# Group sums of the first sequence's v: additions of halves on VectorE in place of sums over a strided axis

## The chip, the cores and the metric

The kernel is one program on one core of a Trainium2 chip. The metric is its time on the device in microseconds (us), the median of the runs. The engines go by short names: TensorE is PE, VectorE is DVE, ScalarE is ACT, GpSimd is POOL, and SyncE is SP, whose queue issues nearly all of the kernel's DMAs.

## The reference

Three layers in a row, in float32: an attention with two parts, a gated MLP and a second MLP. One part of the attention works on means of four neighbouring positions, the other on a band of seven positions around each query.

```python
# 4 batches, 8 heads, 576 positions, 64 channels a head
q_d, k_d, v_d = (t.reshape(B, H, S // 4, 4, D).mean(axis=3) for t in (q, k, v))
out_up = np.repeat(sm_attn(q_d, k_d, v_d), 4, axis=2)      # softmax attention, scale 1/8
scores = scale * np.matmul(q, k.transpose(0, 1, 3, 2))
scores = np.where(np.abs(pos[:, None] - pos[None, :]) < 4, scores, -1e9)
x = out_up + softmax(scores) @ v                           # then to 2304 tokens x 512
g = x @ w_gate                                             # 512 x 1536
x = (g / (1 + np.exp(-g)) * (x @ w_val)) @ w_out           # 1536 x 512
h = x @ w_in                                               # 512 x 2048
out = (np.maximum(h, 0) + alpha * np.minimum(h, 0)) @ w_out2   # 2048 x 512
```

The change touches v_d, the means of four rows of v, for the first of the four batches (the first sequence). The kernel holds them as sums and puts the factor of 1/4 in later.

## The kernel before

**Tiling.** The tokens are cut into 8 blocks of 288, half a sequence each, and the 8 heads into NP = 4 pairs. A half unit n is one block and one pair; there are 32, of which units 0 to 7 (NPRO = 8), the first sequence, run as a prologue. Units 0 to 3 hold the first half of the sequence; n below 4 therefore also names the pair.

**One half unit** goes through these steps, each a function:
- a_T (lines 306 to 334) transposes q and k so that channels lie on partitions and sums groups of four positions; for n = 0 DVE does the latter (lines 327 and 334), for pairs 1 to 3 POOL.
- a_QK (lines 360 and 364) multiplies q and k for the band and for the means; a_EXP (lines 394 and 403, on ACT) takes exponentials, a_NRM divides by the sums (line 427 on ACT for the means).
- a_vd makes vs, the sums of four rows of v, on up to 72 partitions: for n below 4 on DVE, one reduction for each half f of the sequence (line 344), two in a pair, eight in all. In the tile vd a partition holds four rows of 64 channels side by side for each head and half; the reduction reads it in an order in which the four rows are the innermost axis, so neighbouring reads are 64 elements apart. For the later sequences POOL does it by additions of halves (lines 347 and 348), in place in vd and then into vs.
- a_PT (lines 441 and 444) turns the attention weights around, and a_PV (line 461) multiplies them with vs and (line 465) with vw, the windows of v for the band. The windows are copied on the chip's memory into vwin (line 260 and its neighbours) and loaded from there; vw lies in the tile qv. Then ACT scales the product of the means by 1/4 (line 469, the tile is a part of qs), DVE adds both parts (line 470), ACT makes xh, a rounded copy (line 474), and POOL the rest xl (line 475).

The four pairs of the first half have a PSUM bank pair each (att, y0, y1, gv), and units 4 to 7 take over the first three when these are read out.

**The MLPs.** Each product is three matmuls of float32 parts in fp32r (lines 488 to 490: high by high, high by low, low by high). The first MLP has 12 slices j of d_ff, each with a gate, a value and an out weight (g0, v0, o0 and so on; raw_152, raw_154 and raw_156 are those of j = 0, raw_172 to raw_176 those of j = 2, raw_178 to raw_182 those of j = 3, raw_913 to raw_917 those of j = 4). Weights come as 64-bit numbers and are prepared in w_split: two ACT operations (lines 129 and 137), one on DVE (139), a rounding copy on ACT (142) and a subtraction on POOL (143), all 128x512. In block 0 the products of slice j stand behind the preparation of its weights. For a slice, g is projected (m_g), ACT takes a tanh (527), DVE multiplies (528), v is projected (m_v), DVE multiplies again (534), ACT rounds (537), POOL takes the rest (538), and m_y multiplies with the out weight, one slice later. After 8 blocks the second MLP follows (lines 605 to 627).

**Order.** The queues of all five engines are filled by a scheduler. It simulates the program with costs of its own and puts the instructions of each engine in the order in which they come up there. So an instruction with another cost can move others on all queues. A few of them are bound by hand: preparations to instructions of the attention (K's gD, gP, gA), and the copies into vwin for the later sequences to given weight loads. Tiles of the prologue lie in the slots of weights of j = 4 to 11, whose loads therefore wait until the tiles have been read. Once these preparations are over, the products follow one another with the attention of the later blocks in between.

Of the kernel before, what the change touches and what calls it, by code (L numbers as in the profile page):

```python
# [14 lines left out]
AX = mybir.AxisListType  # L15
# [8 lines left out]
def attn_moe_moe2_kernel(  # L24
# [13 lines left out]
    nc = tc.nc  # L38
# [7 lines left out]
    NP = H // 2  # L46
# [99 lines left out]
    hu = {}  # L146
# [4 lines left out]
    vds = {}  # L151
    bds = [ap_.tile([128, 2, NW, 128], F32, name=f"bd{i}", bufs=1) for i in range(NBD)]

    def coords(n):
        blk, hp = divmod(n, NP)
        b, half = divmod(blk, 2)
        return b, half, hp, blk
# [178 lines left out]
    def a_vd(n):  # L336
        b, half, hp, blk = coords(n)
        if n < NPRO and K["vr"]:
            return
        if half == 0:  # L340
            vs = vss[hp] = ap_.tile([72, 2, 2, D], F32, tag=f"vs{hp}", name="vs", bufs=1)
            for f in range(2):
                if n < NP:
                    nc.vector.reduce_sum(vs[:, f], hu[n]["vd"][f].rearrange("p h (r c) -> p h c r", r=4), axis=AX.X)
                    continue
                vv = hu[n]["vd"][f].rearrange("p h (r c) -> p h r c", r=4)
                nc.gpsimd.tensor_tensor(out=vv[:, :, 0:2], in0=vv[:, :, 0:2], in1=vv[:, :, 2:4], op=ALU.add)
                nc.gpsimd.tensor_tensor(out=vs[:, f], in0=vv[:, :, 0], in1=vv[:, :, 1], op=ALU.add)
# [296 lines left out]
    if True:  # L645
# [38 lines left out]
        def a_all(n, A):  # L684
            a_T(n, A)
            if K["vd1"] == 0:
                a_vd(n)
            a_QK(n, A)
            gate(n, 0)
            if K["vd1"] == 1:  # L690
                a_vd(n)
            a_EXP(n)
            a_NRM(n)
            gate(n, 1)
            if K["vd1"] == 2:
                a_vd(n)
            a_PT(n, A)
            if K["vd1"] == 3:
                a_vd(n)
            a_PV(n, A)  # L700
# [67 lines left out]
        for n in range(NPRO, NHU):  # L768
            if n < 2 * NP:
                c = K["c"]  # L770
                p, oT, oE, oP, oV = c * (n - NP) + 1, 1, 1, c - 1, c
            else:
                p, oT, oE, oP, oV = OFF + K["sp"] * (n - 2 * NP), K["oT"], K["oE"], K["oP"], K["oV"]
# [98 lines left out]
```

## Time and profile before

| | |
|---|---|
| time, median of 3 runs | 1009.46 us (1009.44 to 1010.22) |
| span of the profiled execution | 1008.6 us |
| PE busy | 970.5 us, 96% of the span |
| DVE busy | 479.7 us, 48% |
| POOL busy | 380.0 us, 38% |
| ACT busy | 307.6 us, 30% |

The profile comes from one execution whose instructions lie within a span of 1008.6 us; the time of a run is counted by the device and has what lies around the span in it. Busy times are those in which an engine executes; an instruction that waits for another engine or for a DMA is not counted. The table is an average over the whole program: the stages at its beginning look different, and the rows below are from there. In a row of the timeline, square brackets hold the time that the engine stood idle just before, and what ended that.

### The profile page before, as it was taken

The numbers are of one execution on the slowest core, as the hardware profiler recorded it, in microseconds if no ns is written. First come the engines' busy times: TensorE is split into PE (matmuls) and PEld (weight loads), VectorE is DVE, ScalarE is ACT, GpSimd is POOL, SyncE is SP. The second block draws the span as 40 slices with busy tenths as digits, with TensorE's granted clock in tenths as the row PEclk, the third lists the DMA queues.
The fourth block names the chain that finished last, engine by engine and source line by source line (L and its number), as shares of the span: only waits on it lengthen the run. The fifth ranks groups of instructions, "written<-read, shape, count | busy, mean of one in ns | idle before, by whom it ended". The sixth has DMA issues, their size and how long they took to land.

```text
span 1008.6 us, 19231 instructions
## 1 busy us (share of the span) xinstructions
PE 970.5 (96%) x7760; PEld 866.4 (86%) x7760; DVE 479.7 (48%) x1010; ACT 307.6 (30%) x699; POOL 380.0 (38%) x488
## 2 busy tenths in 40 slices
PE   5689899999999999999999999999999999999998
PEld 4488799999999999999999997888888888888897
DVE  5886874464535464545432769623222222322232
ACT  4598632222222222222223656312111111211111
POOL 6487852244322334222223436624223222322222
PEclk9799999999999999999999999999999999999999
DMA  7899731132111221111104883102000100100010
GB/s 185 254 337 340 174 89 35 27 82 56 41 38 33 70 45 41 44 23 21 41 9 141 287 255 106 32 1 79 6 0 21 53 1 1 47 7 0 1 43 21
DMA packets 135888, 77.80 MB, mean 77 GB/s; under 512 B 97401, under 2 KB 127097, under 8 KB 135033
## 3 DMA queue, kind: packets, MB, share of 16 engines
q1 hardware_dynamic: 135735, 76.57, 26.9%
q8 instruction: 60, 0.98, 0.4%
q14 instruction: 29, 0.24, 0.1%
q10 hardware_dynamic: 64, 0.01, 0.0%
HBM read 67.12 MB, written 15.73 MB: 82 GB/s over the span
## 4 chain that ended last, share of the span: by engine, by line
PE 81%; DMA 7%; DVE 4%; SPq 3%; POOL 2%; ACT 2%; issue 1%; POOLq 0%; DVEq 0%; ACTq 0%
PE y L625 7%; PE y L627 7%; PE y L626 7%; PE g L488 6%; PE v L489 6%; PE v L488 6%; PE g L489 6%; PE g L490 6%; PE v L490 5%; PE y L488 4%; PE y L490 4%; PE y L489 4%; PE h L488 3%; PE h L490 3%; PE h L489 3%; DMA raw<-in_moe_w_out_dram 3%
## 5 line engine op out<-in xcount | busy, mean ns | idle before, releaser
L613 POOL TENSOR_TENSOR gl<-t,gh 128x512 fp32r<-128x512 f32 (+1 forms) x80 | 97.1, 1214 | 250.6 <-ACT gh L612 244.3
L612 ACT CAST gh<-t 128x512 fp32r<-128x512 f32 (+1 forms) x80 | 46.1, 578 | 278.5 <-DVE t L609 238.8
L488 PE MATMUL g<-xh,w 128*128 128x288 f32 x384 | 117.7, 306 | 10.4 <-DVE u L528 5.4
L490 PE MATMUL g<-xh,w 128*128 128x288 f32 x384 | 115.0, 300 | 0.8 <-POOL qT L294 0.8
L488 PE MATMUL v<-xh,w 128*128 128x288 f32 x384 | 115.7, 301 | 0.1
L489 PE MATMUL v<-xl,w 128*128 128x288 f32 x384 | 115.1, 300 | 0.0
L489 PE MATMUL g<-xl,w 128*128 128x288 f32 x384 | 114.8, 299 | 0.0
L489 PE MATMUL y<-pl,w 128*128 128x288 f32 x384 | 113.9, 299 | 0.8 <-POOL pl L538 0.8
L625 PE MATMUL y<-w,gh 128*128 128x512 f32 x288 | 113.2, 393 | 1.0 <-ACT sy L557 1.0
L490 PE MATMUL v<-xh,w 128*128 128x288 f32 x384 | 113.3, 295 | 0.0
L490 PE MATMUL y<-ph,w 128*128 128x288 f32 x384 | 113.0, 297 | 0.0
L626 PE MATMUL y<-w,gh 128*128 128x512 f32 x288 | 112.8, 392 | 0.0
L627 PE MATMUL y<-w,gl 128*128 128x512 f32 x288 | 112.0, 392 | 0.0
L528 DVE SCALAR_TENSOR_TENSOR u<-u,g 128x288 f32<-128x288 f32 x96 | 43.3, 451 | 143.0 <-ACT u L527 142.9
L488 PE MATMUL y<-ph,w 128*128 128x288 f32 x384 | 110.9, 302 | 0.0
L538 POOL TENSOR_TENSOR pl<-u,ph 128x288 fp32r<-128x288 f32 x96 | 81.6, 850 | 56.9 <-ACT ph L537 56.5
L143 POOL TENSOR_TENSOR w<-st,w 128x512 fp32r<-128x512 f32 x52 | 70.7, 1366 | 55.6 <-ACT w L142 55.3
L488 PEld LDWEIGHTS g<-xh,w 128*128 128x128 f32 x384 | 73.3, 191 | 14.2 <-DVE u L528 7.4
L607 DVE TENSOR_SCALAR t<-h,alpha 128x512 f32<-128x512 f32 (+1 forms) x40 | 27.9, 696 | 110.7 <-PE h L490 109.5
L488 PEld LDWEIGHTS y<-ph,w 128*128 128x128 f32 x384 | 70.8, 189 | 4.5 <-issue 4.4
L490 PEld LDWEIGHTS g<-xh,w 128*128 128x128 f32 x384 | 73.6, 192 | 1.1 <-POOL qT L294 1.1
L527 ACT ACTIVATE u<-g 128x288 f32<-128x288 f32 x96 | 39.3, 409 | 115.4 <-PE g L490 109.3
(197 smaller groups left out, 2148.2 us busy)
## 6 DMA issues: line engine op xcount, KB each, us to landing
raw<-in_moe_w_out_dram SPq DMA_DIRECT2D x28, 512.0 KB
raw<-in_moe_w_in_dram SPq DMA_DIRECT2D x16, 512.0 KB
raw<-in_moe_w_gate_dram SPq DMA_DIRECT2D x12, 512.0 KB
raw<-in_moe_w_val_dram SPq DMA_DIRECT2D x12, 512.0 KB
vw<-vwin SPq DMA_DIRECT2D x48, 96.0 KB
out_dram<-os SPq DMA_DIRECT2D x18, 256.0 KB
sy<-y SPq DMA_DIRECT2D x16, 256.0 KB
y<-ys SPq DMA_DIRECT2D x14, 288.0 KB
```

The costliest lines, as they stand in the source:

```text
L143: eng.tensor_sub(w[:, 1], st, f32(w[:, 0]))
L488: nc.tensor.matmul(o, lhi, rhi, start=first, stop=False)
L489: nc.tensor.matmul(o, lhi, rlo, start=False, stop=False)
L490: nc.tensor.matmul(o, llo, rhi, start=False, stop=last)
L527: nc.scalar.activation(out=u, in_=GV[0][:, :HB], func=AF.Tanh, scale=0.5)
L528: nc.vector.scalar_tensor_tensor(out=u, in0=u, scalar=1.0, in1=GV[0][:, :HB], op0=ALU.add, op1=ALU.mult)
L538: nc.gpsimd.tensor_sub(pl, u, f32(ph))
L612: nc.scalar.copy(out=gh[:, :n], in_=t[:, :n])
L613: nc.gpsimd.tensor_sub(gl[:, :n], t[:, :n], f32(gh[:, :n]))
L625: nc.tensor.matmul(o, gh[:, ms], ohi, start=(j == 0), stop=False)
L626: nc.tensor.matmul(o, gh[:, ms], olo, start=False, stop=False)
L627: nc.tensor.matmul(o, gl[:, ms], ohi, start=False, stop=(j == F2 - 1))
```

## The change

For the first sequence (n below NP) the eight reductions go out. In their place DVE makes two additions for each pair of heads, over both halves f at once: the first adds rows 2 and 3 of each group of four to rows 0 and 1 in place in vd (512 results a partition), the second adds the two sums and writes vs (256 results a partition). These are four times two instructions in place of four times two. POOL's additions for the later sequences are as before. Lines after 344 have numbers higher by 3 in the changed kernel: 469 becomes 472, 474 becomes 477.

```diff
--- before.py
+++ after.py
@@ -339,10 +339,13 @@
             return
         if half == 0:
             vs = vss[hp] = ap_.tile([72, 2, 2, D], F32, tag=f"vs{hp}", name="vs", bufs=1)
+            if n < NP:
+                vv = vds[hp].rearrange("p h f (r c) -> p (h f) r c", r=4)
+                nc.vector.tensor_add(vv[:, :, 0:2], vv[:, :, 0:2], vv[:, :, 2:4])
+                vv = vds[hp].rearrange("p h f (r c) -> p f h r c", r=4)
+                nc.vector.tensor_add(vs, vv[:, :, :, 0], vv[:, :, :, 1])
+                return
             for f in range(2):
-                if n < NP:
-                    nc.vector.reduce_sum(vs[:, f], hu[n]["vd"][f].rearrange("p h (r c) -> p h c r", r=4), axis=AX.X)
-                    continue
                 vv = hu[n]["vd"][f].rearrange("p h (r c) -> p h r c", r=4)
                 nc.gpsimd.tensor_tensor(out=vv[:, :, 0:2], in0=vv[:, :, 0:2], in1=vv[:, :, 2:4], op=ALU.add)
                 nc.gpsimd.tensor_tensor(out=vs[:, f], in0=vv[:, :, 0], in1=vv[:, :, 1], op=ALU.add)
```

The scheduler gives out another order on all five engines from the additions on until about 145 us of the kernel before; from there on the orders agree.

On ACT, behind pair 3's exponentials in the prologue, before (qs_215, qs_268 and qs_323 belong to pairs 0, 1 and 2, xh_505 is block 0's input to the MLP, st2 the weights of j = 0 under preparation):

```order
L469 ACTIVATE qs_215<-att_68 128x72
L469 ACTIVATE qs_268<-y0_69 128x72
L474 CAST xh_505<-qs_215 128x288
L474 CAST xh_505<-qs_268 128x288
L427 ACTIVATE qs_378<-qs_378,sr3_84 72x144 x2
L129 ACTIVATE st2_575<-raw_152 128x512
L137 ACTIVATE st2_575<-raw_152 128x512
L129 ACTIVATE st2_582<-raw_154 128x512
L137 ACTIVATE st2_582<-raw_154 128x512
L129 ACTIVATE st2_589<-raw_156 128x512
L137 ACTIVATE st2_589<-raw_156 128x512
L469 ACTIVATE qs_323<-y1_70 128x72
```

The same place on ACT in the changed kernel:

```order
L430 ACTIVATE qs_378<-qs_378,sr3_84 72x144 x2
L129 ACTIVATE st2_575<-raw_152 128x512
L137 ACTIVATE st2_575<-raw_152 128x512
L129 ACTIVATE st2_582<-raw_154 128x512
L137 ACTIVATE st2_582<-raw_154 128x512
L472 ACTIVATE qs_215<-att_68 128x72
L129 ACTIVATE st2_589<-raw_156 128x512
L137 ACTIVATE st2_589<-raw_156 128x512
L142 CAST w_579<-st2_575 128x512
L472 ACTIVATE qs_268<-y0_69 128x72
L142 CAST w_586<-st2_582 128x512
L477 CAST xh_505<-qs_215 128x288
```

The scaling copies and casts of pairs 0 and 1 have moved behind the first two operations on the weights g0 and v0, and the casts of these weights now lie among them.

On SP, from the loads of j = 4 on, before (raw_1516 is the out weight of j = 11, vwin's 192 and 176 rows are the copies of windows for the third and fourth sequence):

```order
L106 DMA raw_913<-in_moe_w_gate_dram 128x4x256
L106 DMA raw_915<-in_moe_w_val_dram 128x4x256
L747 DMA alpha_73<-in_moe2_alpha_dram 128x16x1
L104 DMA raw_1516<-in_moe_w_out_dram 128x1024
L260 DMA vwin_64<-in_v_dram 192x2048
L104 DMA raw_917<-in_moe_w_out_dram 128x1024
L106 DMA raw_921<-in_moe_w_val_dram 128x4x256
L104 DMA raw_923<-in_moe_w_out_dram 128x1024
L260 DMA vwin_64<-in_v_dram 176x2048
```

The same place on SP in the changed kernel:

```order
L750 DMA alpha_73<-in_moe2_alpha_dram 128x16x1
L106 DMA raw_913<-in_moe_w_gate_dram 128x4x256
L104 DMA raw_1516<-in_moe_w_out_dram 128x1024
L260 DMA vwin_64<-in_v_dram 192x2048
L260 DMA vwin_64<-in_v_dram 176x2048
L106 DMA raw_915<-in_moe_w_val_dram 128x4x256
L260 DMA vwin_64<-in_v_dram 15x2048
L283 DMA vwin_64<-in_v_dram 16x108
L104 DMA raw_917<-in_moe_w_out_dram 128x1024
L284 DMA vwin_64<-in_v_dram 16x20
L106 DMA raw_921<-in_moe_w_val_dram 128x4x256
L104 DMA raw_923<-in_moe_w_out_dram 128x1024
```

The value weight of j = 4 (raw_915) has moved behind the copies of 192 and of 176 rows.

On ACT, around the tanh of the first gate product (u_980 from g_621), before (raw_174 and raw_176 are v2 and o2; qs_623, qs_697 and qs_769 belong to half units 4, 5 and 6):

```order
L394 ACTIVATE qs_697,sr1_82<-y0_69,nb_734 72x144 x2
L129 ACTIVATE st2_1007<-raw_174 128x512
L137 ACTIVATE st2_1007<-raw_174 128x512
L427 ACTIVATE qs_623<-qs_623,sr0_81 72x144 x2
L142 CAST w_1004<-st2_1000 128x512
L129 ACTIVATE st2_1014<-raw_176 128x512
L137 ACTIVATE st2_1014<-raw_176 128x512
L527 ACTIVATE u_980<-g_621 128x288
L427 ACTIVATE qs_697<-qs_697,sr1_82 72x144 x2
L444 COPY qs_623<-att_68 72x288
L142 CAST w_1011<-st2_1007 128x512
L129 ACTIVATE st2_1065<-raw_178 128x512
```

The same place on ACT in the changed kernel:

```order
L406 ACTIVATE qs_697<-qs_697 128x2x96
L129 ACTIVATE st2_1065<-raw_178 128x512
L137 ACTIVATE st2_1065<-raw_178 128x512
L142 CAST w_1018<-st2_1014 128x512
L430 ACTIVATE qs_623<-qs_623,sr0_81 72x144 x2
L397 ACTIVATE qs_769,sr2_83<-y1_70,nb_806 72x144 x2
L430 ACTIVATE qs_697<-qs_697,sr1_82 72x144 x2
L129 ACTIVATE st2_1072<-raw_180 128x512
L137 ACTIVATE st2_1072<-raw_180 128x512
L406 ACTIVATE qs_769<-qs_769 128x2x96
L142 CAST w_1069<-st2_1065 128x512
L530 ACTIVATE u_980<-g_621 128x288
```

The tanh now stands behind the first operations on the weights g3 and v3 and behind line 397 (394 before) and 406 (403) of half unit 6.

## Rows read from the trace of the kernel before

**Rows 1.** Busy time of each engine by stage, PE clock, DMA share, GB/s
```profile
24.00:34.00 10.00, 6.38 (x65) 5.44 (x66) 9.21 (x15) 2.56 (x10) 1.18 (x6) 1.00 0.61 153
34.00:47.00 13.00, 6.18 (x134) 4.35 (x133) 9.24 (x18) 10.12 (x24) 6.64 (x10) 0.66 1.01 305
47.00:60.00 13.00, 9.52 (x108) 8.36 (x109) 12.40 (x33) 12.38 (x33) 11.35 (x15) 0.76 1.03 322
60.00:80.00 20.00, 19.90 (x212) 18.53 (x211) 16.09 (x36) 16.85 (x43) 17.07 (x18) 0.95 0.96 348
80.00:130.00 50.00, 43.21 (x394) 39.44 (x393) 38.99 (x68) 37.60 (x76) 42.09 (x39) 0.97 0.83 238
150.00:540.00 390.00, 389.71 (x4116) 371.01 (x4116) 189.92 (x502) 98.83 (x262) 121.56 (x208) 1.00 0.19 42
```

**Rows 2.** DVE in order of time: start us, us, line, out<-in, count, idle before
```profile
24.30 7.76 DVE L344 TENSOR_REDUCE vs<-vd 72x128 f32<-72x512 f32 x8
...
32.24 0.45 DVE L470 TENSOR_TENSOR qs<-att,qs 128x288 f32<-128x288 f32 x1
...
38.27 0.45 DVE L334 TENSOR_REDUCE qs<-qs 128x72 f32<-128x288 f32 x1
39.44 0.69 DVE L139 SCALAR_TENSOR_TENSOR st<-st 128x512 int32<-128x512 int32 x1 [0.73 <-ACT st L137]
...
104.66 1.68 DVE L139 SCALAR_TENSOR_TENSOR st<-st 128x512 int32<-128x512 int32 x1 [0.41 <-ACT st L137]
```

**Rows 3.** PE in order of time, the same columns, 25 to 59 us
```profile
25.39 0.51 PE L461 MATMUL att<-qs,vs 72*64 72x72 f32 x4 [2.15 <-DVE vs L344]
...
28.35 0.58 PE L465 MATMUL att<-bd,qv 128*64 128x96 f32 x2 [1.49 <-DMA qv<-vwin]
...
33.25 0.74 PE L315 MATMUL att<-ident,qv 96*128 96x96 f32 x3
...
47.66 0.61 PE L488 MATMUL g<-xh,w 128*128 128x288 f32 x1 [3.03 <-DVE qs L470]
...
58.94 0.61 PE L488 MATMUL g<-xh,w 128*128 128x288 f32 x1 [0.91 <-DVE u L528]
```

**Rows 4.** Chain of waits in order of time, 20 to 40 us: start, length, what
```profile
20.08 9.09 DMA qv<-vwin
...
33.66 5.85 DMA raw<-in_moe_w_out_dram
```

**Rows 5.** ACT in order of time, 30 to 80 us
```profile
30.47 0.23 ACT L469 ACTIVATE qs<-att 128x72 f32<-128x72 f32 x1 [5.22 <-PE att L465]
...
36.39 0.68 ACT L129 ACTIVATE st<-raw 128x512 f32<-128x512 f32 x1 [2.17 <-DMA raw<-in_moe_w_gate_dram]
36.97 0.65 ACT L137 ACTIVATE st<-raw 128x512 int32<-128x512 uint8 x1
38.20 0.66 ACT L129 ACTIVATE st<-raw 128x512 f32<-128x512 f32 x1 [0.57 <-DMA raw<-in_moe_w_val_dram]
...
46.13 0.23 ACT L469 ACTIVATE qs<-gv 128x72 f32<-128x72 f32 x1
...
55.70 0.41 ACT L527 ACTIVATE u<-g 128x288 f32<-128x288 f32 x1
...
71.50 0.67 ACT L129 ACTIVATE st<-raw 128x512 f32<-128x512 f32 x1 [1.34 <-DMA raw<-in_moe_w_out_dram]
...
79.46 0.68 ACT L129 ACTIVATE st<-raw 128x512 f32<-128x512 f32 x1 [1.57 <-DMA raw<-in_moe_w_gate_dram]
```

**Rows 6.** ACT by line, 30 to 80 us: count, busy us, mean ns, idle before
```profile
L129 ACT ACTIVATE st<-raw 128x512 f32<-128x512 f32 x17 | 11.6, 681 | 6.4 <-DMA raw<-in_moe_w_gate_dram 4.4 <-DMA raw<-in_moe_w_out_dram 1.3 <-DMA raw<-in_moe_w_val_dram 0.6
...
L142 ACT CAST w<-st 128x512 fp32r<-128x512 f32 x15 | 9.2, 625 | 0.0
...
L474 ACT CAST xh<-qs 128x288 fp32r<-128x288 f32 x7 | 3.1, 438 | 0.6 <-DVE qs L470 0.6
```

**Rows 7.** PE in order of time, the last of the late stalls
```profile
125.54 0.40 PE L488 MATMUL g<-xh,w 128*128 128x288 f32 x1 [0.76 <-ACT w L142]
```

## The prediction, made before the changed kernel ran

> **What bounds the kernel now.** I read the table by stage first. In 150 to 540 us TensorE (PE) is busy 389.71 of 390 us [rows 1], so the end moves only if PE reaches that solid stretch earlier or later. PE's open time lies ahead of it: 3.62 + 6.82 + 3.48 = 13.9 us of idleness in 24 to 60 us, 0.1 in 60 to 80, and 6.79 in 80 to 130. The clock column adds what idleness doesn't show: 0.66 and 0.76 of full speed in 34 to 47 and 47 to 60 [rows 1].
>
> Then the edited instruction. The eight reductions of line 344 fill VectorE (DVE) from 24.30 for 7.76 us, 0.97 us each [rows 2]. PE waits 2.15 us for the first of them, at 25.39 [rows 3]. But what came next shows that this wait costs nothing: PE waits again, until 28.35, for the window loads into qv [rows 3], and the chain of waits between 20 and 40 us runs through DMA: qv<-vwin until 20.08 + 9.09 = 29.17, then the first expert weights until 33.66 + 5.85 = 39.51 [rows 4]. Line 344 isn't in it.
>
> **The change, part 1: the arithmetic.** Out go 8 x 0.97 = 7.76 us. In come four in-place additions with 512 results per partition and four with 256. No row has an f32 addition of this size on DVE. Nearest for 512 is line 139, two SBUF inputs, 128x512: 0.69 us with GpSimd idle, 1.68 with GpSimd at work; for 256 it is line 470, 288 elements, 0.45 us [rows 2]. GpSimd has 1.18 us of work in 24 to 34 us [rows 1], so I take the low end, 4 x 0.65 + 4 x 0.36 = 4.0 us, a little under the rows because DVE's rows overlap by some 0.1. The far end is 4 x 1.68 + 4 x 0.84 = 10.1 us. The last group sum is ready near 28.4 us instead of 32.06.
>
> Line 344 needs 0.97 us for 512 elements that lie apart, 1.9 ns each; line 334 needs 0.45 us for 288 that lie side by side, 1.6 ns each [rows 2]. The Trainium skill (SBUF — State Buffer, section "Door 1: The DMA port swizzle") says that an access which crosses into a new 16-byte line every time pays for it; by it the additions, which read rows of 64, would be at the low end of my bounds. The trace agrees in direction only.
>
> Taken alone the saving is hidden: the window loads land at 29.17 all the same, and PE has work from there to the transposes of 33.25 [rows 3]. Alone it is worth 0.
>
> **Part 2: the order.** The scheduler rearranges all five queues from here to about 145 us; after that they agree row for row. So one number decides: where PE stands at 145 us. I follow it with durations of before.
>
> *ScalarE (ACT), 30 to 49 us.* Before, the scaling copy of pair 0 (line 469) runs at 30.47 and pair 1's soon after, and ACT then waits until gate weight 0 lands at 36.39 [rows 5]. After, both copies stand behind the weight work of gate 0 and value 0. Value 0's starts at 38.20, on landing [rows 5], and takes 1.13 us (lines 129 and 137, 0.68 and 0.65 less the overlap of 0.1 that 36.39 and 36.97 show), so pair 0's copy runs at 39.4, 8.9 us later. Its addition on DVE goes from 32.24 [rows 2] to 40.0, its bank comes free then, and the transposes of q for pairs 4 to 6 go from 33.25 to 40.5 and later. From 36.39 on ACT is the pace. Before pair 3's copy (46.13) it now has in addition two copies (0.11 each), two casts of xh (0.33), one weight's work (1.13) and one cast of 0.52, and lacks 0.71 us of line 394 [rows 5, 6]: +1.8, so 48.0. DVE then does a weight operation (0.6) and pair 3's addition (0.4) and ends at 49.0. That addition is what the first projection waited for at 47.66 [rows 3]: g0 starts at about 49.05.
>
> *The second projection.* g1 starts at 58.94 after a wait for line 528 [rows 3], which follows ACT's tanh of 55.70 [rows 5]. The new order has 5.4 us more of ACT work in front of that tanh: weight work of g3 and v3 (2 x 1.13), three casts (3 x 0.52) and 1.6 us of lines 394, 403 and 427 for pairs 5 and 6. With the 0.9 us of copies and casts moved out of ACT's idle time above, the tanh comes at 62.0 and g1 at 62.8: +3.9 us. PE then still owes pair 4's products (0.9 us), so it is 4.8 us behind. Slow-clock stretches after the idle ones are there before and after, and I let them cancel.
>
> *SyncE.* Value weight 4 now follows out weight 11 and the window copies of the last two sequences (192 and 176 rows of 8 KB). Before, out weight 4 had gate 4, value 4, out weight 11 and the 192 rows ahead of it and landed at 71.50 [rows 5]. Value 4 after has the 176 rows more (1.4 MB) and one weight less (0.5 MB): 0.9 MB at the 348 GB/s of 60 to 80 us [rows 1] is 2.6 us, so it lands near 74, or 72 if the queue drains faster behind copies. ACT reaches it at 69 and holds it ahead of the next products' casts, so PE loses 0 to 3 us. With 1 it is some 5.5 us behind at 80 us (4 to 8).
>
> *80 to 145 us.* PE idles 6.79 us here [rows 1], mostly in five stalls of 0.76 to 1.14 us from 97 to 126, each released by ACT or DVE, as the last one at 125.54 by a weight's cast [rows 7]. PE waits there for the weights' preparation, and a PE that is late fits into these gaps. So what counts is how late the preparation is. In both orders ACT waits for gate 5, which has the same bytes ahead of it and landed at 79.46 [rows 5]; there the new order still owes 2.2 us of ACT work that before had done (tanh and cast of one tile, lines 394, 403 and 427 of pair 7). I take 2.2, and 0.8 for gate 11, which now stands behind key loads that wait for DVE and is what PE waits for at 125.54: **+3.0 us**. Bounds: all absorbed, 0; nothing absorbed, 5.5 to 7.5.
>
> After 145 us a shift stays a shift, since PE is busy without gaps.
>
> **The sum.** Part 1 gives 0, part 2 +3.0. The profiled execution spans 1008.6 us and the median of the runs is 1009.46; the 0.9 us between them lie outside the span and stay. The span becomes 1011.6, the time 1012.5 us.
>
> **Rivals.**
> 1. *The gaps swallow it.* If DMA arrival alone sets the stalls of 97 to 126 us, neither preparation nor PE is late: 1009.5. For it: DMA is 0.96 busy in 60 to 80 us and 0.83 in 80 to 130 [rows 1]. Against: ACT and DVE release these stalls.
> 2. *Nothing is swallowed.* Value 4 lands at 74 or later, ACT stands still for 5 us with the next tile's cast behind it, and new stalls replace the old: 5.5 to 7.5, 1015 to 1017. It decides when ACT idles over 4 us ahead of value 4.
> 3. *The other side: faster.* DVE is free 3.7 us sooner, pair 3's normalization and products end sooner, and the first projection starts sooner by all of it: 1009.46 - 3.7 = 1005.8. It needs pair 3 to wait for DVE alone. Against: ACT idles 5.22 us before 30.47 and 2.17 before 36.39, the latter for DMA [rows 5], so what follows waits for weights. The same time would come if the new order fitted PE's late gaps better by chance. The Trainium skill (VectorE: DVE Perf Modes, section "Rules for kernel authors") calls the reduction VectorE's slowest operation and worth restructuring on a hot path; that rule points to this rival, and no row shows this path to be the hot one.
> 4. *The additions are no faster*, 10.1 us against 7.76: the last sum comes at 34.5, still before the weights of 36.39, and nothing moves by it.
>
> **How the numbers follow.** Forecast (+1.5 to +4.5) 0.38, rival 2 0.18, rivals 1 and 4 0.24, rival 3 0.20. The likeliest is 1012.5. A range of 1006 to 1017 leaves out half of rival 3 and the far end of rival 2, under 0.2. A measurement tells about 0.2%, 2 us, from no change. Slower by more: rival 2 and most of the forecast, 0.5; within: the rest of the forecast and rivals 1 and 4, 0.3; faster by more: 0.2.
>
> **What would show it.** Right: eight DVE rows of 0.6 to 0.7 and 0.3 to 0.4 us from 24.3, done by 28.6; pair 0's copy on ACT at 39 and not at 30; g0 near 49, g1 near 62 to 63; ACT waiting for value 4's DMA near 70; less than 6.8 us of idle PE in 80 to 130; lines after 150 us as long as before. Wrong: g1 before 59, or PE at 145 us where it stood before.

## The result

The changed kernel takes 1015.39 us (median of 5 executions, 1014.17 to 1017.84) against 1009.46 us; the ratio is 1.0055, with a 95% interval of 1.0043 to 1.0068. It is slower by 0.55%, some 5.6 us by the ratio and 5.9 between the medians.

Its profiled execution spans 1012.1 us, 3.5 us more than that of the kernel before. The other 2.4 us between the medians are not in these two spans. The five executions of the changed kernel span 1012.0 to 1014.5 us, median 1013.0, so the profiled one is near the best of them, and their times lie 2.4 us above the span in the median. In 33 later executions of the kernel before the time lies 1.9 us above the span in most; taken off the 1009.46 us, this leaves a span of some 1007.6 us (an estimate), so the profiled one of before, at 1008.6, was a long one for that occasion.

### The profile page after: what moved, and what is told of

The parts are those of the page before. It is cut to its first block, busy times and chain, and to the rows that moved or that the text cites. A ratio compares the mean times of both kernels' runs of the same rounds, so it can differ in the third digit from the quotient of the medians.

```text
span 1012.1 us, 19229 instructions
## 1 busy us (share of the span) xinstructions
PE 969.3 (96%) x7760; PEld 867.1 (86%) x7760; DVE 478.4 (47%) x1010; ACT 307.9 (30%) x699; POOL 378.7 (37%) x488
## 4 chain that ended last, share of the span: by engine, by line
PE 82%; DVE 5%; DMA 4%; ACT 3%; POOL 2%; issue 2%; SPq 0%; DVEq 0%; ACTq 0%; POOLq 0%
PE y L628 7%; PE y L630 6%; PE y L629 6%; PE g L491 6%; PE v L492 6%; PE v L491 6%; PE g L493 6%; PE g L492 6%; PE v L493 6%; PE y L491 4%; PE y L493 4%; PE y L492 4%; PE h L491 3%; PE h L493 3%; PE h L492 3%
## 5 line engine op out<-in xcount | busy, mean ns | idle before, releaser
L541 POOL TENSOR_TENSOR pl<-u,ph 128x288 fp32r<-128x288 f32 x96 | 79.0, 823 | 57.7 <-ACT ph L540 57.2
L491 PEld LDWEIGHTS g<-xh,w 128*128 128x128 f32 x384 | 73.6, 192 | 13.0 <-DVE u L531 10.6
L492 PEld LDWEIGHTS v<-xl,w 128*128 128x128 f32 x384 | 73.3, 191 | 1.7
```

Of the source, the lines that this page charges most:

```text
L491: nc.tensor.matmul(o, lhi, rhi, start=first, stop=False)
L492: nc.tensor.matmul(o, lhi, rlo, start=False, stop=False)
L541: nc.gpsimd.tensor_sub(pl, u, f32(ph))
```

## The profile after

The table by stage has the columns of [rows 1]: stretch, its length, busy us of PE, PE's weight loads, DVE, ACT and POOL, PE's granted clock, DMA share, GB/s.

```profile
24.00:34.00 10.00, 4.96 (x64) 4.57 (x64) 5.95 (x17) 1.55 (x6) 0.92 (x5) 1.00 0.75 195
34.00:47.00 13.00, 7.19 (x181) 5.22 (x181) 8.28 (x15) 11.29 (x25) 7.26 (x7) 0.55 1.05 302
47.00:60.00 13.00, 7.13 (x49) 5.68 (x38) 11.51 (x28) 11.40 (x33) 11.42 (x18) 0.76 0.86 270
60.00:80.00 20.00, 15.86 (x188) 14.67 (x188) 14.28 (x30) 16.31 (x38) 13.63 (x15) 0.77 1.02 353
80.00:130.00 50.00, 46.80 (x381) 44.91 (x381) 42.69 (x74) 37.31 (x81) 42.34 (x39) 0.93 0.83 234
150.00:540.00 390.00, 390.00 (x4163) 371.20 (x4162) 191.29 (x505) 99.19 (x262) 121.40 (x209) 1.00 0.18 41
```

DVE is busy for 5.95 us in 24 to 34 us, where it was 9.21 [rows 1]. PE is busy for 7.13 instead of 9.52 us in 47 to 60, and for 15.86 instead of 19.90 in 60 to 80, at 0.77 of the full clock there instead of 0.95. In 80 to 130 us it is busier than before, 46.80 against 43.21. In 150 to 540 us nothing has changed.

DVE's rows of the additions, in the columns of [rows 2]:

```profile
24.14 2.49 DVE L344 TENSOR_TENSOR vd<-vd 72x512 f32<-72x512 f32 x4
...
26.81 1.42 DVE L346 TENSOR_TENSOR vs<-vd 72x256 f32<-72x256 f32 x4
```

They take 0.62 and 0.36 us each, 3.9 us in all in place of 7.76. PE's rows, as in [rows 3]:

```profile
27.27 0.75 PE L464 MATMUL att<-qs,vs 72*64 72x72 f32 x8 [4.20 <-DVE vs L346]
...
38.34 0.74 PE L315 MATMUL att<-ident,qv 96*128 96x96 f32 x3 [6.11 <-DMA raw<-in_moe_w_gate_dram]
...
48.84 0.61 PE L491 MATMUL g<-xh,w 128*128 128x288 f32 x1 [0.99 <-DVE qs L473]
...
58.27 0.63 PE L444 MATMUL att<-ident,qs 72*72 72x72 f32 x4 [4.07 <-ACT qs L430]
...
64.49 0.61 PE L491 MATMUL g<-xh,w 128*128 128x288 f32 x1 [4.14 <-DVE u L531]
...
121.21 0.61 PE L491 MATMUL g<-xh,w 128*128 128x288 f32 x1 [2.90 <-DVE u L531]
```

PE waits 4.20 us for the first sums of all, since the scheduler put all four first additions ahead of the second ones. It then waits for ACT's work on the first weights before it may transpose pairs 4 to 6 (38.34, before 33.25 [rows 3]). The row names the weights' DMA; what frees the bank att is pair 0's addition on DVE, which follows ACT's copy of 37.10 (below) and ends 0.05 us before the transposes start:

```profile
37.84 0.45 DVE L473 TENSOR_TENSOR qs<-att,qs 128x288 f32<-128x288 f32 x1
```

PE also waits three times for ACT and DVE: ahead of the first gate product, of the transposes at 58.27 and of the second product, which starts at 64.49 instead of 58.94. A last stall of 2.90 us stands at 121.21. On ACT (columns of [rows 5]):

```profile
34.53 0.66 ACT L129 ACTIVATE st<-raw 128x512 f32<-128x512 f32 x1 [5.18 <-DMA raw<-in_moe_w_gate_dram]
...
37.10 0.21 ACT L472 ACTIVATE qs<-att 128x72 f32<-128x72 f32 x1
...
61.59 0.43 ACT L530 ACTIVATE u<-g 128x288 f32<-128x288 f32 x1
...
70.78 0.23 ACT L472 ACTIVATE qs<-att 128x72 f32<-128x72 f32 x1 [1.93 <-PE att L468]
...
72.36 0.68 ACT L129 ACTIVATE st<-raw 128x512 f32<-128x512 f32 x1
...
116.63 0.62 ACT L142 CAST w<-st 128x512 fp32r<-128x512 f32 x1 [3.66 <-DVE st L132]
...
119.97 0.40 ACT L530 ACTIVATE u<-g 128x288 f32<-128x288 f32 x1
```

Pair 0's copy runs at 37.10 instead of 30.47, behind the weights, and the tanh of the first product at 61.59 instead of 55.70 [rows 5]. Value weight 4 (72.36) is not waited for; ACT came to it from a wait for PE at 70.78.

## The experiments

All of them rest on one edit, which lays every engine's queue down in a given order. Edges that only fix the order of issue run from each instruction to the next of its engine. In the traces of the kernels pinned to the order of before or of after, the instructions of ACT, DVE, POOL and SP come in the order of the kernel named.

```diff
+def pin(tc, orders):
+    traced = list(tc.nc.cur_bb.bb.instructions)
+    edge = mybir.DependencyInfo(mybir.DependencyClass.NoSync, mybir.DependencyReason.DATA)
...
+            if last is not None:
+                tc.add_manual_dep(traced[at], last.name, edge, reason="pin")
...
         attn_moe_moe2_kernel(tc, *args)
+        pin(tc, ORDERS)
```

ORDERS holds a list of numbers for each engine. The diffs below write "before" and "after" for the lists read from the two programs. Times are given as ratios to the kernel before, whose executions were made in turn with them on the same chip; one thousandth is 1.0 us.

### Arithmetic or order

The kernel before, without an edit:

> The kernel before once more, for what two traces of one program differ by. Both theories: 1009.5 us, span 1008.6 +- 0.4, and 0.9 us between span and time. If instead the stalls of 600 us or the time outside the span wander by 1 us from one execution to the next here too, then 1 us of the changed kernel's loss is not of the change.

Measured: ratio 1.0001 (0.9992 to 1.0010), median 1010.78, spans of 1007.2 to 1009.9 us. Some 2 us of difference between two profiles therefore mean nothing. This also goes for 1.4 of the 3.5 us between the spans of before and after, which arise late: from the tanh of a gate product near 403 us to the second MLP's first output product (line 625 or 628, at 618 to 626 us) it is 215.14 us in the profile before and 216.56 in the profile after, but 215.0 to 215.9 in this one and in those of the eleven kernels below, whatever their order.

The additions, all queues in the order of before:

```diff
+ORDERS = {"PE": before, "DVE": before, "Activation": before, "Pool": before, "SP": before}
```

> The additions, with every engine's queue held in the order of the kernel before (the additions stand where the reductions stood). Theory 'it is the order': the 3.9 us saved on VectorE are hidden behind the window loads and the first weights, so 1009.5 +- 1 us, first gate product at 47.7 us. Rival 'it is the arithmetic' (the additions hold something up that the reductions did not): 1015 us. Rival 'the saving counts and only the order hides it': 1005.6 us, first gate product at 44.

Measured: 0.9994 (0.9985 to 1.0004). DVE and then PE:

```profile
24.29 0.68 DVE L344 TENSOR_TENSOR vd<-vd 72x512 f32<-72x512 f32 x1
25.00 0.42 DVE L346 TENSOR_TENSOR vs<-vd 72x256 f32<-72x256 f32 x1
25.35 0.68 DVE L344 TENSOR_TENSOR vd<-vd 72x512 f32<-72x512 f32 x1
...
29.92 0.46 DVE L473 TENSOR_TENSOR qs<-att,qs 128x288 f32<-128x288 f32 x1 [1.06 <-ACT qs L472]
```

```profile
47.83 0.61 PE L491 MATMUL g<-xh,w 128*128 128x288 f32 x1 [3.03 <-DVE qs L473]
```

Pair 0's addition of line 473 (470 before) starts at 29.92 instead of 32.24 [rows 2], and yet the first product starts at 47.83 (47.66 before): the saving is hidden, as it was argued, and the additions by themselves do no harm.

The reductions in the order of after:

```diff
+ORDERS = {"PE": after, "DVE": after, "Activation": after, "Pool": after, "SP": after}   # in the kernel before
```

> The other corner: the reductions of the kernel before, with every queue in the order of the changed kernel. 'It is the order': 1015.4 +- 1.5 us, since the last reduction at 32 is still ahead of the first weights at 34.5 us. 'It is the arithmetic': 1009.5 us. 'The saving counts': 1019 us.

Measured: 1.0032 (1.0021 to 1.0044). A loss comes with the order, without the change's arithmetic, though it is 3.2 us, where some 6 were expected. It is the order, then, for the greater part at least. That the reductions are 2 us better in it than the additions (1.0055, taken on another occasion) is at the edge of the intervals and stays open; a difference between their traces stands below the table.

The additions in the new order, with SP's queue as before:

```diff
+ORDERS = {"PE": after, "DVE": after, "Activation": after, "Pool": after, "SP": before}
```

> The changed kernel with the queue of SyncE alone put back into the order of before; the other four engines keep the new order. 'The new order of ScalarE, VectorE and GpSimd makes the loss': second gate product still at 64 us, time 1014 to 1016. 'The new order of the transfers makes it (value weight 4, later gate weight 11)': 1010 to 1011.5 us, and the stall of 2.9 us at 121 us is gone.

Measured: 1.0064 (1.0051 to 1.0076). PE has the same two stalls:

```profile
65.97 0.61 PE L491 MATMUL g<-xh,w 128*128 128x288 f32 x1 [4.14 <-DVE u L531]
...
122.42 0.40 PE L491 MATMUL g<-xh,w 128*128 128x288 f32 x1 [2.36 <-DVE u L531]
```

The order of the transfers is not the cause; putting it back gains nothing.

### Which stretch of the order

Here the order of one kernel holds up to the instruction named, and what is left then follows in the order of the other.

```diff
+ORDERS = {e: after[e] up to the tanh of product 4, then before[e] for e in engines}
```

> The additions; every queue in the new order up to the tanh of gate product 4 (about 85 us), in the order of before from there on. The new order's late start of the products (5 to 8 us at products 1 to 4) is all in. Early theory (the copies and casts behind the weights cost time that is not made good): 2 to 5 us over the kernel before. Late theory (the loss is made by the new order behind 85 us, the early delay is swallowed by the gaps of 97 to 126 us): 0 +- 1 us.

```diff
+ORDERS = {e: before[e] up to the tanh of product 4, then after[e] for e in engines}
```

> The counterpart: the order of before up to the tanh of gate product 4, the new order behind it. Early theory: 0 to 1 us over the kernel before, with product 1 at 59 us. Late theory: 3 to 6 us over it, with a stall of 2 to 3 us ahead of gate product 10. If both this and its counterpart come out within 1 us, only the two together lose, and the loss is of neither part.

Measured: 1.0059 (1.0045 to 1.0072) for the new order in front, 0.9996 (0.9984 to 1.0007) for the new order behind. All of the loss is made ahead of 85 us, and with the order of before behind it the gaps do not swallow it. The late order, which I suspected after the profile of after with its stall at 121 us, costs nothing when PE arrives in time.

```diff
+ORDERS = {e: after[e] up to the tanh of product 8, then before[e] for e in engines}
```

> New order up to the tanh of gate product 8 (109 us), order of before behind it. In the changed kernel product 8 came 1.6 us ahead of the kernel before, and all of the loss came behind it. Late theory: 0 to 2 us below the kernel before, if the lead is kept. Early theory: 2 to 5 us over it, since the new order has used up VectorE's and GpSimd's room for the weights by then, whatever stands behind.

```diff
+ORDERS = {e: before[e] up to the tanh of product 8, then after[e] for e in engines}
```

> Order of before up to the tanh of gate product 8, new order behind it. Late theory, if the cause lies between products 8 and 11 (VectorE held for 4 us in line 131, the tanh of product 9 behind it): 3 to 6 us over the kernel before, stall of 2 to 3 us ahead of product 10. Late theory with the cause between products 4 and 8: 0 to 1 us. Early theory: 0 to 1 us.

Measured: 1.0041 (1.0025 to 1.0057) and 1.0013 (1.0002 to 1.0024). The lead at product 8 is not kept, and again it is the front that loses.

### Which part of the early order

```diff
+ORDERS = {e: after[e] up to the first gate product, then before[e] for e in engines}
```

> The additions; new order up to the first gate product, order of before from there. This keeps the copies and casts of pairs 0 to 2 behind the first weights' work (first product 1.2 to 2.4 us late) and puts the tanh of product 0 back ahead of the work on the fourth slice's weights. Theory 'the tanh': 0 to 1.5 us over the kernel before. Theory 'the copies': 4 to 6 us over it.

```diff
+ORDERS = {e: before[e] up to the first gate product, then after[e] for e in engines}
```

> The counterpart: order of before up to the first gate product, new order from there, so the copies are early and the tanh late. 'The tanh': product 0 at 47.8 us, product 1 at 62 to 64, time 3 to 5 us over the kernel before. 'The copies': 0 to 1 us over it.

Measured: 1.0051 (1.0038 to 1.0065) for the first, 1.0028 (1.0017 to 1.0039) for the second. The order ahead of the first product makes nearly the whole loss by itself; I had expected 0 to 1.5 us of it, and 3 to 5 of the rest. The two add up to 7.9 us and give 5.6 together, so each covers a part of the other.

That within the first part it is the copies is read from its trace, not from a run that moves them alone. On ACT:

```profile
35.90 0.66 ACT L129 ACTIVATE st<-raw 128x512 f32<-128x512 f32 x1 [6.00 <-DMA raw<-in_moe_w_gate_dram]
...
38.46 0.22 ACT L472 ACTIVATE qs<-att 128x72 f32<-128x72 f32 x1
...
59.44 0.72 ACT L430 ACTIVATE qs<-qs,sr 72x144 f32<-72x144 f32 x2 [1.57 <-DVE sr L419]
...
61.53 0.68 ACT L129 ACTIVATE st<-raw 128x512 f32<-128x512 f32 x1 [0.57 <-POOL w L143]
```

The weights land at 35.90, within 0.5 us of before. Pair 0's copy stands behind them (38.46), so the banks come free later. Pairs 4 to 6 are transposed later for it and normalized later, and at 59.44 ACT waits 1.57 us for pair 5's sums, with the weights of slice 3 behind it. These start at 61.53, after 0.57 us more of waiting for POOL; in the kernel before:

```profile
57.44 0.69 ACT L129 ACTIVATE st<-raw 128x512 f32<-128x512 f32 x1
```

From there to 113 us ACT's weight work stays 2 to 5 us late. PE's late stalls, in this kernel and then in the kernel before (with [rows 7] for the third):

```profile
50.02 0.61 PE L491 MATMUL g<-xh,w 128*128 128x288 f32 x1 [1.01 <-DVE qs L473]
...
116.96 0.40 PE L491 MATMUL g<-xh,w 128*128 128x288 f32 x1 [1.14 <-DVE st L131]
...
123.13 0.40 PE L491 MATMUL g<-xh,w 128*128 128x288 f32 x1 [0.99 <-DVE u L531]
...
130.31 0.40 PE L491 MATMUL g<-xh,w 128*128 128x288 f32 x1 [0.76 <-ACT w L142]
```

```profile
112.19 0.40 PE L488 MATMUL g<-xh,w 128*128 128x288 f32 x1 [1.14 <-DVE st L131]
...
118.36 0.40 PE L488 MATMUL g<-xh,w 128*128 128x288 f32 x1 [0.99 <-DVE u L528]
```

They are the same three stalls with the same 1.14, 0.99 and 0.76 us, each 4.77 us later. (The second profile of the kernel before has the first of them, 1.15 us at 112.65, and not the other two, so this rests on two executions that match.) This is how the gaps come to swallow nothing in this kernel: ACT takes its queue in order, the weights' work stands in it behind the late attention and the products' tanh, and what PE waits for in the gaps is late by as much as PE.

The tanh by itself, in the new order; on ACT (on DVE its multiplication, line 531, likewise goes ahead by fourteen):

```diff
 L397 ACTIVATE qs_697,sr1_82<-y0_69,nb_734 72x144 x2
+L530 ACTIVATE u_980<-g_621 128x288
 L142 CAST w_1011<-st2_1007 128x512
...
 L142 CAST w_1069<-st2_1065 128x512
-L530 ACTIVATE u_980<-g_621 128x288
 L129 ACTIVATE st2_1079<-raw_182 128x512
```

> The changed kernel with two instructions moved: the tanh of product 0 on ScalarE goes ahead by sixteen instructions (some 6 us of work), its multiplication on VectorE by fourteen. 'The tanh': product 1 starts at 60 to 61 us instead of 64 to 66, and 3 to 4 of the 5.7 us come back, so 1 to 3 us over the kernel before. 'The copies', or the rest of the new order: 4.5 to 6 us over it.

```diff
+ORDERS = {e: before[e] up to the first gate product, then after[e] with the tanh moved ahead for e in engines}
```

> Both undone: order of before up to the first gate product, then the new order with that tanh and its multiplication moved ahead. If the two places are the whole loss: 0 +- 1 us against the kernel before. If something else of the new order between 50 and 85 us loses too: what is left over 1 us is its share.

Measured: 1.0032 (1.0019 to 1.0046), and 1.0034 (1.0021 to 1.0047) with the copies early as well. In the new order the move brings some 2 us (from 1.0055, another occasion); with the copies early it brings nothing (1.0028 without it). PE in the first of the two:

```profile
59.69 0.76 PE L444 MATMUL att<-ident,qs 72*72 72x72 f32 x4 [4.32 <-ACT qs L430]
...
61.53 0.59 PE L491 MATMUL g<-xh,w 128*128 128x288 f32 x1
...
66.14 0.61 PE L491 MATMUL v<-xh,w 128*128 128x288 f32 x1 [1.38 <-DVE u L537]
```

The second gate product no longer waits, but the value product behind it waits for line 537, which I had left in its place, and PE still stood 4.32 us ahead of the transposes at 59.69. So the tanh is one of several things that hold PE between 54 and 66 us, and mending it alone settles little. What else in the new order behind the first product loses the 2.8 us is open.

How late the tanh of a product comes, in us, against the second profile of the kernel before (starts of line 530 less those of line 527; one execution each, whereas the ratios are medians):

| kernel | 0 | 1 | 3 | 4 | 6 | 8 | 10 | 24 (block 2) | ratio |
|---|---|---|---|---|---|---|---|---|---|
| before, first profile | 0.0 | 0.1 | -0.5 | -0.4 | -0.5 | -0.5 | -1.1 | -1.0 | |
| after | 5.9 | 3.9 | 7.2 | 5.3 | 4.1 | -2.1 | 4.0 | 1.1 | 1.0055 |
| new to product 0 | 1.8 | 4.2 | 4.2 | 2.9 | 2.9 | 4.3 | 4.4 | 3.4 | 1.0051 |
| new to product 4 | 7.2 | 5.2 | 8.6 | 6.6 | 4.6 | 5.0 | 5.1 | 4.6 | 1.0059 |
| new to product 8 | 5.8 | 3.7 | 6.4 | 4.5 | 3.3 | -3.0 | 0.8 | -0.1 | 1.0041 |
| before to product 0 | 5.3 | 3.2 | 7.7 | 5.8 | 4.9 | -1.3 | 4.4 | 1.5 | 1.0028 |
| before to product 4 | -0.4 | 0.1 | 0.1 | -1.3 | 1.8 | -4.4 | -0.4 | -1.8 | 0.9996 |
| new, SP as before | 7.4 | 5.3 | 9.0 | 7.0 | 5.9 | -0.4 | 6.1 | 5.4 | 1.0064 |
| reductions, new | 7.6 | 5.5 | 9.6 | 7.6 | 6.5 | 0.8 | 4.6 | 2.5 | 1.0032 |

With the order of before behind, most of the delay runs through. With the new order behind, it is made good at product 8, where the weights' work stands ahead of the tanh, and is back at product 10.

Part of what brings it back shows in line 131 of DVE, a step in the preparation of a weight between products 8 and 9. In all five traced kernels that have the additions and the new order from the first product to beyond product 9 (after, SP as before, before to product 0, and the two with the tanh moved), it takes 3.99 to 4.02 us there, and the delay grows by 4.0 to 4.4 us from product 8 to product 9. With the reductions in the same order it takes 2.23 us, and the delay grows by 1.1; in every other kernel it stays below that. It isn't the whole: in the kernel that is new to product 8 the delay grows by 3.2 without it. No run tests whether this makes the 2 us between additions and reductions in the new order.

## Why the prediction was right, and where it was not

The time lies in the range and on the side forecast. By size it is past the forecast's own bounds (1.5 to 4.5 us): 5.6 us, which is what rival 2 gave, though not by rival 2's mechanism, since ACT did not wait for value weight 4; the range held because it took in most of rival 2. The runs bear out that the arithmetic is hidden and that the new order makes PE late ahead of its solid stretch. The terms of the sum fared worse, and it is in part luck that they came near: 5.5 us were forecast at 80 us, and the profile has 7.2 and 5.3 at products 3 and 4, from errors on both sides.

- **Part 1** was right: 3.9 us of additions against 4.0, worth nothing at the end (0.9994 with the order of before). The Trainium skill (VectorE: DVE Perf Modes, "Rules for kernel authors") calls the reduction the slowest operation of VectorE and advises restructuring on a hot path. The rows agree on the price (0.97 us for a reduction against 0.62 and 0.36); this path was not the hot one.
- **The first product**, +1.4: mis-sized. In the profile it comes at 48.84, close to the 49.05 forecast, but the weights had landed at 34.53 there, 1.9 us ahead of the profile before. From the weights' arrival to the product it is 14.3 us after, and 14.1 in the kernel that has the new order up to there alone (35.90 to 50.02); before it is 11.3 (36.39 [rows 5] to 47.66 [rows 3]). So the term is some 2.9 us. ACT's part was right: pair 3's copy comes 11.9 us behind the weights, and 11.6 were forecast. Most of what is missing lies behind that copy. DVE's weight operation ahead of pair 3's addition took 1.75 us, with POOL at work, and I had counted 0.6, although [rows 2] has 1.68 for line 139:

```profile
46.47 0.23 ACT L472 ACTIVATE qs<-gv 128x72 f32<-128x72 f32 x1
46.67 1.75 DVE L139 SCALAR_TENSOR_TENSOR st<-st 128x512 int32<-128x512 int32 x1 [0.68 <-POOL xl L478]
48.34 0.45 DVE L473 TENSOR_TENSOR qs<-gv,qs 128x288 f32<-128x288 f32 x1
```

- **The second product**, +3.9: it was 5.6 (64.49 against 58.94). The tanh came at 61.59, as forecast (62.0), but the product 2.9 us behind it and not 0.8. On DVE the multiplication stood behind a weight's operation of 1.73 us and a normalization:

```profile
61.88 1.73 DVE L139 SCALAR_TENSOR_TENSOR st<-st 128x512 int32<-128x512 int32 x1
...
63.99 0.45 DVE L531 SCALAR_TENSOR_TENSOR u<-u,g 128x288 f32<-128x288 f32 x1
```

- **"Slow-clock stretches cancel"** was wrong. By four us each, after and then the second profile of before:

```profile
56.00:60.00 4.00, 1.03 (x7) 0.60 (x8) 3.49 (x11) 4.00 (x14) 3.90 (x5) 0.89 0.73 236
60.00:64.00 4.00, 0.35 (x3) 0.10 (x2) 3.86 (x9) 4.00 (x10) 1.72 (x2) 0.50 0.99 373
64.00:68.00 4.00, 3.51 (x14) 3.51 (x15) 3.93 (x10) 3.20 (x8) 3.31 (x4) 0.50 1.02 352
68.00:72.00 4.00, 4.00 (x55) 3.72 (x55) 1.12 (x3) 1.50 (x6) 2.58 (x2) 0.83 0.97 304
```

```profile
56.00:60.00 4.00, 3.29 (x31) 2.82 (x32) 3.72 (x9) 4.00 (x14) 2.60 (x3) 0.75 1.01 244
60.00:64.00 4.00, 4.00 (x40) 3.72 (x39) 2.70 (x8) 4.00 (x12) 3.79 (x4) 0.83 0.62 181
64.00:68.00 4.00, 3.39 (x71) 2.82 (x71) 3.96 (x9) 4.00 (x12) 3.43 (x4) 1.00 0.94 356
```

PE worked for 1.03 of the four us from 56 and for 0.35 of those from 60; the granted clock is 0.50 in 60 to 68, the lower of its two levels (1.2 GHz), and PE runs its late products at it: 3.5 us of work at half speed and four at 0.83 lose 2.4 us. With the little work of 56 to 64 this makes some 2.7 us, against some 1.5 before (3.29 us at 0.75 and four at 0.83), so 1.2 us do not cancel; these are estimates from busy time and mean clock. Here a stall cost its own length and a slow stretch behind it.
- **Value weight 4**, +1: it cost nothing; ACT was itself held by PE (70.78) and then found the weight there. (4.8 and 1 make 5.8, and the prediction went on with 5.5.)
- **The gaps**: I let 2.5 of 5.5 us disappear in them because the weights' work would be only 2.2 us late. That PE's delay follows the weights' work was right; how late that work is was wrong, and it depends on the order behind. In the order of before it is nearly as late as PE, and most of the delay stays: 4.6 of 6.6 us from product 4 to 24 in the kernel that is new to product 4, and 3.4 of 4.2 from product 1 in the one that is new to product 0. In the new order it is on time at product 8, and PE is ahead there, but the last weights are then late: ACT waits 3.66 us for line 132, which follows line 131, and the tanh of product 9 comes behind that (116.63 and 119.97, shown above). Even so, only 1.1 of 5.3 us are left at product 24 in the profile of after (2.1 of 5.7 against the first profile of before). That is less than the 3.0 forecast.
- **Where the rest of the 5.9 us is**: of the 3.5 us between the two profiles, 2.1 stand ahead of product 24 and 1.4 behind 403 us, where no other kernel loses more than 0.8. The other 2.4 are between the profiles and the medians: 0.9 because the profiled execution of after is near the best, 1.0 (an estimate) because that of before is a long one, and 0.5 outside the spans. No slower execution of the changed kernel was traced, so which term is short in a median one stays open. The two that the trace shows short ahead of 80 us are the projections' and the clock's.
- **Between span and time** lie 1.9 us in the kernel before and not 0.9: I had set the median of the runs against a span that wasn't that of the median run. The sum doesn't suffer, since it adds 3.0 to the measured 1009.46.

Rival 1 (nothing late but DMA) falls with the time and with the stalls that moved by 4.77 us, rival 3 (the saving counts) with 0.9994, and rival 4 (the additions no faster) with 3.9 against 7.76 us. No version here beats the kernel before by more than its interval; the lowest, 0.9994 and 0.9996, are the same time.

## What to carry to other kernels

Where a scheduler lays down the order, an edit has two prices: that of its instructions and that of the order that comes out. Fix the order by hand and run the edit, and what it replaces, in both: the four times tell how much of the difference is the order's.

On an engine that takes its queue in order, a small copy that frees a bank is worth what waits for the bank. By the trace of the kernel that is new to product 0 (1.0051), two copies of 0.2 us that went behind the work on the first weights started its loss, since the weight work behind them came 2 to 5 us later; no run moved the copies alone. Idle time later in the program absorbs a delay only if what ends that idle time is not late as well.

## What the runs showed of the hardware

- An addition that reads what the one before it wrote starts 0.71 us after it (24.29 and 25.00 above); independent ones of the same size start 0.62 us apart (2.49 / 4 in the profile after). Alternating the two steps takes 1.06 us for a pair (24.29 to 25.35), 4.2 for four; all first steps and then all second ones took 3.9.
- Line 131, at its shortest 0.38 us in the profile of after and 0.65 at 121.07, takes 3.99 at 111.29. On DVE, and then GpSimd's operations at that time, one upon the other:

```profile
111.29 3.99 DVE L131 TENSOR_SCALAR st<-st 128x512 int32<-128x512 int32 x1
...
121.07 0.65 DVE L131 TENSOR_SCALAR st<-st 128x512 int32<-128x512 int32 x1
```

```profile
110.41 1.28 POOL L143 TENSOR_TENSOR w<-st,w 128x512 fp32r<-128x512 f32 x1
...
111.69 2.54 POOL L143 TENSOR_TENSOR w<-st,w 128x512 fp32r<-128x512 f32 x2
114.19 0.80 POOL L541 TENSOR_TENSOR pl<-u,ph 128x288 fp32r<-128x288 f32 x1
```

Line 131 ends at 115.28, 0.3 us behind the last of them. The Trainium skill (SBUF — State Buffer, "SBUF: two separate sides") says that VectorE and GpSimd share a pair of ports, which one instruction of GpSimd, or of VectorE in a two-port mode or with two SBUF inputs, holds to its end while the other engine is blocked. The trace agrees, as far as line 131 is such an instruction, which no row tells: it ended only behind the last of GpSimd's operations, and not between two of them.
- The granted clock in 44 to 48 us was 0.50 in one profile of the kernel before and 1.00 in the other. The first product came 11.3 and 11.2 us behind the first weights in both: PE worked for only 0.97 and 1.04 us of these four and waited for others, so here its clock was of no account.
